# Scores written to the opposite partition half, and a strided unit's products alternated with newer scores

## The chip, the cores and the metric

The kernel runs on one core of a Trainium2 chip. The metric is device time in microseconds for one execution. Several executions are timed, and one more is recorded by the hardware profiler; line numbers such as L316 are lines of the kernel before, unless a text says that they are those of the changed kernel.

## The reference

The reference computes sparse attention for 8 batches of 8 heads (576 positions, head dimension 64), and feeds the result, as 4608 tokens of 512 values, to a two-layer network with g = h·cos(h) between the layers.

```python
def _attn_ref(q, k, v):
    stride = 32
    scores = scale * np.matmul(q, k.transpose(0, 1, 3, 2))
    mask_local = (rel >= 0) & (rel < stride)
    mask_strided = (rel >= 0) & (pos[None, :] % stride == pos[:, None] % stride)
    masks = np.stack([mask_local if h < H // 2 else mask_strided for h in range(H)], axis=0)
    ...
    return np.matmul(attn, v)

def _moe_ref(x, w_in, w_out):
    h = x @ w_in
    g = h * np.cos(h)
    return g @ w_out
```

Four heads of a batch are local: a query sees the 32 newest positions. Four are strided: a query sees the earlier positions of its own residue modulo 32.

## The kernel before

**The network** is most of the work. Tokens are taken in 12 blocks of 384 (j), the hidden width of 2048 in 16 chunks of 128 (f). A chunk's first layer is 12 matmuls into the tile h (L358), its second layer 9 matmuls into three accumulators acc (L382); the second layer of a chunk is issued three chunks after its first layer (LAG). Between them ACT, DVE and POOL make g_hi and g_lo from h (L364 to L375). All inputs of a block come from xT, a scratch in HBM that the attention writes.

**Attention** is cut into units, ten for each batch. For each pair of heads there are two strided units and three local ones. A unit has three steps on TensorE, separated by yield in the code:

- scores: q times k into the scores bank (L290 strided, L249 local), then the softmax on DVE, POOL and ACT, which ends with POOL's product into pn_s or e_sb (L225);
- transposes: three matmuls with an identity (L302 strided, L257 local), then ACT copies them to pt;
- products: v times pt into the products bank (L316 strided, L265 local), then ACT copies them to x_t (L322, L328) or x_l, from where a DMA takes them to xT.

All these matmuls have fp32 operands. A strided unit holds six groups of 54 positions (the second unit of a pair of heads holds five): 12 or 10 score matmuls and 12 or 10 product matmuls. A local unit has 6 and 6.

**Partition halves.** A score matmul contracts over the 64 values of a head, so it reads one half of the partitions: half 0 (0 to 63) or half 1 (64 to 127). A local unit has one head in each half (j); a strided unit has even groups in half 0 and odd groups in half 1 (i). Before, the scores are written to the same half as they are read from. The products of a strided unit read the 54 keys of head j from half j and write half j. The products of a local unit read 96 partitions, across both halves, and write half j. A matmul that reads from half a and writes half b is said below to be in quarter (a,b): before, all scores and all strided products are in (0,0) or (1,1).

**What sets the order.** Batches 0 and 1 come first, together with the loading of the weights (`plain` units). There a scheduler in the build decides the order on every engine. The other six batches, 60 units, are laid between the network's chunks from token block 2 on. There every matmul is chained to the one before it (in_turn, L147), so that TensorE's order is the order of the code. Before chunk n the units that fall due there (KNOTS, L58) form a burst: for unit k the transposes of unit k-2, then the products of unit k-3, then the scores of unit k (schedule, L416). In this part there is one bank of PSUM for scores, one for transposes and one for products. Of ten bursts for a batch, four have the products of a strided unit: their scores are those of the pair's last strided unit once (10 matmuls) and of local units three times (6 matmuls).

Of the kernel before, what the change touches and what calls it, by code (L numbers as in the profile page):

```python
# [3 lines left out]

# [17 lines left out]
STRIDE = 32  # L22
DM, DFF = H * D, 2048
NTOK = B * S
P = 128

QB = 64
# [41 lines left out]
def attention_cos_ffn(ctx, tc, qkl, vl, qkvs, w_in, w_out, eye, eye16, mask_l0, mask_l, mask_s, out):  # L69
# [26 lines left out]
        nc.gpsimd.memset(t, 0.0)  # L96
    exps, reduced = [], []

    def order(later, first, reason):
        tc.add_manual_dep(  # L100
            later.ins, first.ins.name,
            mybir.DependencyInfo(mybir.DependencyClass.NoSync, mybir.DependencyReason.DATA), reason=reason,
        )
# [49 lines left out]
        return mm  # L153

    class Attention:

# [77 lines left out]
        def local(self, b, p, u):  # L236
            qk = self.ld.tile([P, QS + KS], F32, name="qk")
            nc.sync.dma_start(out=qk[:, :QKL], in_=qkl[b, p, u])
            v = self.ld.tile([P, VS], F32, name="v", bufs=4)
            nc.sync.dma_start(out=v[:KW], in_=vl[b, p, u])  # L240
            q_t, k_t = qk[:, :LU * QB], qk[:, LU * QB:]
            v_t = v[:KW].rearrange("k (t j d) -> k t j d", j=2, d=D)
            mask = ml0.rearrange("p (t w) -> p t w", w=KW) if u == 0 else ml.unsqueeze(1).broadcast_to([P, LU, KW])
            s_ps = self.score_bank(mask)
            for t in range(LU):
                for j in range(2):
                    rows = slice(64 * j, 64 * j + 64)
                    lo = STRIDE if u + t == 0 else 0
                    self.scored = self.pe(nc.tensor.matmul(  # L249
                        s_ps[rows, t * KW + lo:(t + 1) * KW], q_t[rows, QB * t:QB * (t + 1)],  # L250
                        k_t[rows, QB * t + lo:QB * t + KW], start=not self.plain, stop=True, skip_group_check=True,
                    ))
            pn = self.softmax(s_ps[:, :LU * KW].rearrange("p (t w) -> p t w", w=KW), mask, LU, KW)
            yield
            t_ps = self.bank(self.transposed)
            for t in range(LU):
                self.pe(nc.tensor.transpose(t_ps[:KW, t * P:(t + 1) * P], pn[:, t], ident))  # L257
            pt = self.wk.tile([P, LU * P], F32, name="pt")
            nc.scalar.copy(out=pt[:KW], in_=t_ps[:KW, :LU * P])
            yield  # L260
            x_t = self.wk.tile([P, LU * QB], F32, name="x_l", bufs=4 if self.plain else 2)
            a_ps = self.bank(self.products)
            for t in range(LU):
                for j in range(2):
                    self.pe(nc.tensor.matmul(  # L265
                        a_ps[64 * j:64 * j + 64, t * QB:(t + 1) * QB], v_t[:, t, j],
                        pt[:KW, t * P + 64 * j:t * P + 64 * j + QB], start=True, stop=True, skip_group_check=True,
                    ))
            nc.scalar.copy(out=x_t, in_=a_ps[:, :LU * QB])
            at = b * S + u * LU * QB  # L270
            nc.scalar.dma_start(out=xT[:, 2 + p, at:at + LU * QB], in_=x_t)

        def strided(self, b, p, u):
            real = min(SU, NG - SU * u)
            qk = self.ld.tile([P, QS + KS], F32, name="qk")
            nc.sync.dma_start(out=qk, in_=qkvs[b, p, u, :, :QS + KS])
            v = self.ld.tile([P, VS], F32, name="v", bufs=4)
            nc.sync.dma_start(out=v[:, :real * D], in_=qkvs[b, p, u, :, QS + KS:QS + KS + real * D])
            q_t = qk[:, :QS].rearrange("p (t q) -> p t q", q=GB)
            k_t = qk[:, QS:].rearrange("p (t k) -> p t k", k=GB)  # L280
            v_t = v.rearrange("p (t d) -> p t d", d=D)

            mask = ms.unsqueeze(1).broadcast_to([P, SU, GB])
            s_ps = self.score_bank(mask)
            for t in range(SU):
                for i in range(2):
                    if SU * u + t // 2 * 2 + i >= NG:
                        continue
                    rows = slice(64 * i, 64 * i + 64)
                    self.scored = self.pe(nc.tensor.matmul(  # L290
                        s_ps[64 * i:64 * i + GB, t * GB:(t + 1) * GB], q_t[rows, t], k_t[rows, t],
                        start=not self.plain, stop=True, skip_group_check=True,
                    ))
            pn = next(self.pn_s)
            self.softmax(
                s_ps[:, :SU * GB].rearrange("p (t w) -> p t w", w=GB), mask,
                SU, GB, pn[:, :, :GB],
            )
            yield
            t_ps = self.bank(self.transposed)  # L300
            for t in range(0, SU, 2):
                self.pe(nc.tensor.transpose(  # L302
                    t_ps[:, t * GP:(t + 2) * GP], pn[:, t:t + 2].rearrange("p t k -> p (t k)"), ident
                ))
            pt = self.wk.tile([P, LU * P], F32, name="pt")
            nc.scalar.copy(
                out=pt[:, :SU * GB].rearrange("p (t q) -> p t q", q=GB),
                in_=t_ps[:, :SU * GP].rearrange("p (t q) -> p t q", q=GP)[:, :, :GB],
            )
            yield  # L310
            x_t = self.stage((b, p))
            a_ps = self.bank(self.products)
            for t in range(real):
                for j in range(2):
                    keys = slice(64 * j, 64 * j + GB)
                    self.pe(nc.tensor.matmul(  # L316
                        a_ps[64 * j:64 * j + 64, t * GB:(t + 1) * GB], v_t[keys, t],
                        pt[keys, t * GB:(t + 1) * GB], start=True, stop=True, skip_group_check=True,
                    ))
            x_v = x_t.rearrange("p (a r) -> p a r", r=STRIDE)  # L320
            full = min(real, STRIDE // GR - SU * u)
            nc.scalar.copy(  # L322
                out=x_v[:, :, GR * SU * u:GR * (SU * u + full)].rearrange("p a (t r) -> p t a r", r=GR),
                in_=a_ps[:, :full * GB].rearrange("p (t a r) -> p t a r", a=A, r=GR),
            )
            if full < real:
                left = STRIDE % GR
                nc.scalar.copy(  # L328
                    out=x_v[:, :, STRIDE - left:],
                    in_=a_ps[:, full * GB:real * GB].rearrange("p (a r) -> p a r", r=GR)[:, :, :left],  # L330
                )
            if u == NSU - 1:
                nc.scalar.dma_start(out=xT[:, p, b * S:(b + 1) * S], in_=x_t)
# [79 lines left out]
                steps.setdefault(stage, []).append(unit)  # L413
        return steps

    def schedule(units, begun, lag):  # L416


        steps = {}
        for k, at in enumerate(begun):  # L420
            steps.setdefault(at, []).extend(units[m] for m in (k - lag, k - lag - 1, k) if 0 <= m < len(units))
        return steps

    def step(steps, n):
        for unit in steps.get(n, ()):
            next(unit, None)

    with ExitStack() as loading:
        cv = loading.enter_context(tc.tile_pool(name="cv", bufs=2))
        with ExitStack() as stack:  # L430
# [17 lines left out]

            keep_busy(BUSY[0], None)
            for n in range(max(steps) + 1):  # L450
                step(steps, n)
                if n + 1 < len(BUSY):
                    keep_busy(BUSY[n + 1], att.scored)
                if n == LOADS[0]:
                    x0 = load_x(0)
                if n == LOADS[1]:
                    x1 = load_x(1)
# [21 lines left out]
    with ExitStack() as stack:  # L479
        op = stack.enter_context(tc.tile_pool(name="op", bufs=3, reuse_waits="tile"))  # L480
        ps = stack.enter_context(tc.tile_pool(name="ps", bufs=1, space=bass.MemoryType.PSUM, reuse_waits="tile"))
        att = Attention(stack, False, *(((ps, f"acc{i}"),) for i in range(3)), ld_bufs=2)
        units = [unit for b in range(2, B) for unit in att.units(b)]
        begun = np.interp(range(len(units) + UNIT_LAG + 1), [n for _, n in KNOTS], [at for at, _ in KNOTS])
        steps = schedule(units, begun.astype(int).tolist(), UNIT_LAG)
        for n in range(LAG, (NTB - 2) * NFC):
            j, f = 2 + n // NFC, n % NFC
            if f == 0:
                cur, acc = nxt, accumulators(ps_o)
            step(steps, n)  # L490
            if f == LOAD_AT and j + 1 < NTB:
                nxt = load_x(j + 1)
            chunk(j, f, cur, acc)
        while pend:
            outer(*pend.pop(0))
# [97 lines left out]
```

## Time and profile before

| | us |
|---|---|
| median of 3 runs | 1000.85 (1000.22 to 1001.1) |
| the profiled execution's own time | 999.46 |
| its span, first to last instruction | 997.7 |
| first layer's matmuls (L358), busy | 267.9 + 259.7 + 259.4 |
| second layer's matmuls (L382), busy | 227.4 + 224.2 + 224.6 |
| strided products (L316), busy, 704 records | 27.8 |
| local products (L265), busy, 576 records | 27.0 |
| local scores into acc banks (L249), 64 and 96 columns, busy | 4.2 + 25.8 |
| strided scores into acc banks (L290), busy, 572 records | 21.1 |

Busy times of a line are a union of its records, and matmuls overlap, so the rows of this table add up to more than the span. PE is TensorE's matmuls and PEld its weight loads; each matmul of fp32 operands appears as two records of each. The start of a record is measured; its end is modelled, so the text works with the distance from one start to the next. In a timeline, records of one line that follow one another are merged, with their count behind an x.

### The profile page before, as it was taken

The page shows a single profiled execution, that of the slowest core. Times are in us where ns is not written, and L with a number is a line of the kernel's source. Part 1 is how long each engine was busy: PE and PEld are TensorE (multiplying, and loading weights), DVE is VectorE, ACT ScalarE, POOL GpSimd, SP SyncE. Part 2 cuts the span into 40 slices and gives each one's busy share as a digit, 9 for nine tenths or more (in the row PEclk, how much of TensorE's full clock was granted, in tenths as well). Part 3 has the DMA queues.
Part 4 walks back from the last instruction along what each step waited for, and adds up shares of the span by engine and source line. Part 5 has one row for each costly group of instructions (what it writes and reads, how often), then busy time and mean ns, then how long its engine had stood idle before and what let it go on. Part 6 is the DMA issues. An engine that isn't in the chain of part 4 may idle for free.

```text
span 997.7 us, 17749 instructions
## 1 busy us (share of the span) xinstructions
PE 968.3 (97%) x6890; PEld 847.5 (85%) x6890; DVE 466.5 (47%) x1005; ACT 499.2 (50%) x1043; POOL 385.2 (39%) x418
## 2 busy tenths in 40 slices
PE   8988988998999999999999999999999999999998
PEld 5777877877888888888888888888888888889997
DVE  6866677655454444434344444444344444322222
ACT  3655555565555555455445545554454544433433
POOL 2555554544344344333333344434243333332221
PEclk9999999999899999999999999999999999999999
DMA  8963333232322222111211322211221310100000
GB/s 247 300 199 103 111 108 112 80 105 73 102 85 88 70 79 84 42 50 59 83 58 35 110 79 76 82 50 53 88 59 34 98 55 29 41 20 1 33 1 32
DMA packets 48228, 80.14 MB, mean 80 GB/s; under 512 B 5904, under 2 KB 33296, under 8 KB 48144
## 3 DMA queue, kind: packets, MB, share of 16 engines
q1 hardware_dynamic: 38208, 69.35, 23.1%
q10 hardware_dynamic: 9936, 9.65, 2.8%
q8 instruction: 54, 0.88, 0.4%
q14 instruction: 30, 0.25, 0.1%
HBM read 60.11 MB, written 18.87 MB: 79 GB/s over the span
## 4 chain that ended last, share of the span: by engine, by line
PE 78%; DMA 4%; DVE 2%; ACT 1%; issue 1%; POOL 0%; DVEq 0%; POOLq 0%; ACTq 0%; SPq 0%
PE h L358 35%; PE acc L382 34%; DMA raw<-in_w_out 2%; PE acc L249 2%; PE acc L265 2%; PE acc L316 2%; PE acc L290 2%; PE acc L257 1%; PE acc L302 1%; DVE raw L116 1%; DMA raw<-in_w_in 1%; DMA xT<-x_t 0%; ACT r L368 0%; DVE r L371 0%; DVE raw L119 0%
## 5 line engine op out<-in xcount | busy, mean ns | idle before, releaser
L375 POOL TENSOR_TENSOR g_lo<-r,g_hi 128x384 fp32r<-128x384 f32 x192 | 198.3, 1033 | 396.6 <-issue 249.2
L358 PE MATMUL h<-x_hi,wi_h 128*128 128x384 f32 x768 | 267.9, 349 | 13.7 <-DVE r L371 13.7
L358 PE MATMUL h<-x_hi,wi_l 128*128 128x384 f32 x768 | 259.7, 338 | 0.0
L358 PE MATMUL h<-x_lo,wi_h 128*128 128x384 f32 x768 | 259.4, 338 | 0.0
L365 DVE SCALAR_TENSOR_TENSOR r<-r,h 128x384 f32<-128x384 int32 x192 | 106.1, 552 | 270.8 <-ACT r L364 247.7
L382 PE MATMUL acc<-wo_l,g_hi 128*128 128x512 f32 x576 | 227.4, 395 | 0.0
L382 PE MATMUL acc<-wo_h,g_hi 128*128 128x512 f32 x576 | 224.2, 389 | 1.4 <-ACT g_hi L374 1.4
L382 PE MATMUL acc<-wo_h,g_lo 128*128 128x512 f32 x576 | 224.6, 396 | 0.0
L358 PEld LDWEIGHTS h<-x_hi,wi_h 128*128 128x128 f32 x768 | 145.2, 189 | 31.0 <-DVE r L371 19.8
L368 ACT ACTIVATE r<-r,quarter 128x384 f32<-128x384 f32 x192 | 118.5, 617 | 96.5 <-DVE r L365 96.2
L358 PEld LDWEIGHTS h<-x_lo,wi_h 128*128 128x128 f32 x768 | 145.3, 189 | 5.0
L371 DVE TENSOR_TENSOR r<-r,h 128x384 f32<-128x384 f32 x192 | 106.0, 552 | 84.0 <-ACT r L368 83.4
L358 PEld LDWEIGHTS h<-x_hi,wi_l 128*128 128x128 f32 x768 | 145.1, 189 | 0.1
L364 ACT ACTIVATE r<-h 128x384 int32<-128x384 f32 x192 | 93.4, 487 | 102.0 <-PE h L358 95.5
L374 ACT CAST g_hi<-r 128x384 fp32r<-128x384 f32 x192 | 98.3, 512 | 87.5 <-DVE r L371 87.2
L382 PEld LDWEIGHTS acc<-wo_h,g_lo 128*128 128x128 f32 x576 | 108.0, 188 | 22.8
L382 PEld LDWEIGHTS acc<-wo_h,g_hi 128*128 128x128 f32 x576 | 108.3, 188 | 19.0 <-ACT g_hi L374 1.7
L382 PEld LDWEIGHTS acc<-wo_l,g_hi 128*128 128x128 f32 x576 | 108.0, 187 | 18.2
L349 POOL TENSOR_TENSOR x_lo<-x_raw,x_hi 128x384 fp32r<-128x384 f32 x48 | 50.9, 1062 | 130.9 <-DVE x_hi L348 107.4
L214 ACT ACTIVATE e_sb<-t_sb,shift 128x288 f32<-128x288 f32 (+1 forms) x60 | 32.9, 548 | 95.6 <-POOL t_sb L206 95.6
L348 DVE CAST x_hi<-x_raw 128x384 fp32r<-128x384 f32 x48 | 21.6, 452 | 60.9 <-DMA x_raw<-xT 60.2
L206 POOL TENSOR_TENSOR t_sb<-t_sb,mx 128x288 f32<-128x288 f32 (+1 forms) x60 | 41.6, 693 | 16.9 <-DVE mx L205 11.5
(66 smaller groups left out, 855.8 us busy)
## 6 DMA issues: line engine op xcount, KB each, us to landing
qk<-in_qkvs SPq DMA_DIRECT2D x32, 324.0 KB, 3.7
qk<-in_qkl SPq DMA_DIRECT2D x48, 208.0 KB, 3.3
x_raw<-xT SPq DMA_DIRECT2D x48, 192.0 KB, 2.4
out<-o SPq DMA_DIRECT2D x36, 256.0 KB, 2.1
raw<-in_w_in SPq DMA_DIRECT2D x16, 512.0 KB, 3.7
raw<-in_w_out SPq DMA_DIRECT2D x16, 512.0 KB, 3.8
v<-in_vl SPq DMA_DIRECT2D x48, 144.0 KB, 2.2
xT<-x_t ACTq DMA_DIRECT2D x16, 288.0 KB, 3.5
```

Source lines behind the costliest of these rows:

```text
L206: nc.gpsimd.tensor_tensor(out=t, in0=t, in1=mx[:, :n].unsqueeze(2).broadcast_to([P, n, w]), op=ALU.subtract)
L214: nc.scalar.activation(out=e, in_=t, func=AF.Silu, bias=shift1, scale=0.0625)
L348: nc.vector.tensor_copy(out=hi, in_=raw)
L349: nc.gpsimd.tensor_tensor(out=lo, in0=raw, in1=hi.bitcast(F32), op=ALU.subtract)
L358: mm = nc.tensor.matmul(h, w[:, f, c], x[c], start=(i == 0), stop=(i == len(ops) - 1))
L364: nc.scalar.activation(out=k, in_=h, func=AF.Copy, scale=1.0 / (2.0 * math.pi), bias=0.25)
L365: red = nc.vector.scalar_tensor_tensor(out=r, in0=k, scalar=-2.0 * math.pi, in1=h, op0=ALU.mult, op1=ALU.add)
L368: sin = nc.scalar.activation(out=r, in_=r, func=AF.Sin, bias=quarter)
L371: nc.vector.tensor_tensor(out=r, in0=r, in1=h, op=ALU.mult)
L374: nc.scalar.copy(out=g_hi, in_=r)
L375: nc.gpsimd.tensor_tensor(out=g_lo, in0=r, in1=g_hi.bitcast(F32), op=ALU.subtract)
L382: mm = nc.tensor.matmul(acc[t], g[:, ts], w[:, f], start=(f == 0 and i == 0), stop=(f == NFC - 1 and i == 2))
```

## The change

Three edits, all to attention:

- A score matmul that reads half a writes half 1-a, for local and for strided units, in the first two batches too. So all scores are in quarters (0,1) and (1,0). The products then take their columns of pt from where the swapped scores end up after the transposes: the other half's columns for a local unit, those of the neighbouring group (t ^ 1) for a strided one. The products stay in the quarters that they had.
- A unit no longer issues its scores and products itself. It yields a list of them, with a mark that says whether the unit is strided.
- The new function burst takes the place of schedule and step for the last six batches. It issues the transposes as before. If the products are those of a strided unit, it alternates products and scores, matmul by matmul, until one list is used up, and then issues the rest. Otherwise it issues the products and then the scores, as before.

```diff
+    def half(n, rows=64):
+        return slice(64 * n, 64 * n + rows)
...
-            for t in range(LU):
-                for j in range(2):
-                    rows = slice(64 * j, 64 * j + 64)
-                    lo = STRIDE if u + t == 0 else 0
-                    self.scored = self.pe(nc.tensor.matmul(
-                        s_ps[rows, t * KW + lo:(t + 1) * KW], q_t[rows, QB * t:QB * (t + 1)],
...
+            def score(t, j):
+                lo = STRIDE if u + t == 0 else 0
+                self.scored = self.pe(nc.tensor.matmul(
+                    s_ps[half(1 - j), t * KW + lo:(t + 1) * KW], q_t[half(j), QB * t:QB * (t + 1)],
+                    k_t[half(j), QB * t + lo:QB * t + KW], start=not self.plain, stop=True, skip_group_check=True,
+                ))
+
+            yield [partial(score, t, j) for t in range(LU) for j in range(2)], False
...
-                        pt[:KW, t * P + 64 * j:t * P + 64 * j + QB], start=True, stop=True, skip_group_check=True,
...
+                at = t * P + 64 * (1 - j)
+                self.pe(nc.tensor.matmul(
+                    a_ps[half(j), t * QB:(t + 1) * QB], v_t[:, t, j], pt[:KW, at:at + QB], start=True, stop=True,
...
+                    s_ps[half(1 - i, GB), t * GB:(t + 1) * GB], q_t[half(i), t], k_t[half(i), t],
...
+            def product(t, j):
+                at = (t ^ 1) * GB
+                self.pe(nc.tensor.matmul(
+                    a_ps[half(j), t * GB:(t + 1) * GB], v_t[half(j, GB), t], pt[half(j, GB), at:at + GB], start=True,
+                    stop=True, skip_group_check=True,
+                ))
+
+            yield [partial(product, t, j) for t in range(real) for j in range(2)], True
...
+    def burst(transposed, multiplied, scored):
+
+        if transposed:
+            next(transposed)
+        products, small = next(multiplied) if multiplied else ((), False)
+        scores = next(scored)[0] if scored else ()
+        if small:
+            matmuls = [m for pair in itertools.zip_longest(products, scores) for m in pair if m]
+        else:
+            matmuls = [*products, *scores]
+        for matmul in matmuls:
+            matmul()
+        if multiplied:
+            next(multiplied, None)
+        if scored:
+            next(scored)
...
+            for units in bursts.get(n, ()):
+                burst(*units)
```

The first place is TensorE's order in the first burst of the last part that has the products of a strided unit. Here acc_2613, acc_2620 and acc_2456 are the banks of transposes, products and scores, and h and acc_2325 belong to the network. Before:

```order
L382 MATMUL acc_2325<-wo_h,g_lo 128x512
L302 MATMUL acc_2613<-ident,pn_s_97 128x128 x3
L316 MATMUL acc_2620<-pt,v 64x54 x12
L290 MATMUL acc_2456<-qk 54x54 x10
L358 MATMUL h<-x_hi,wi_h 128x384
```

And in the changed kernel, where L327 are the strided products, L297 the strided scores and L371 the first layer:

```order
L313 MATMUL acc_2613<-ident,pn_s_97 128x128 x3
L327 MATMUL acc_2620<-pt,v 64x54
L297 MATMUL acc_2456<-qk 54x54
L327 MATMUL acc_2620<-pt,v 64x54
L297 MATMUL acc_2456<-qk 54x54
...
L327 MATMUL acc_2620<-pt,v 64x54 x2
L371 MATMUL h<-x_hi,wi_h 128x384
```

The two blocks of 12 and 10 have become ten alternations with two products behind them; what stands ahead of and behind the burst is the same.

The second place is TensorE's order in the next burst, whose scores are those of a local unit (two matmuls of 64 columns and four of 96, L254 in the changed kernel):

```order
L313 MATMUL acc_2694<-ident,pn_s_96 128x128 x3
L327 MATMUL acc_2700<-pt,v 64x54
L254 MATMUL acc_2456<-qk 64x64
...
L327 MATMUL acc_2700<-pt,v 64x54
L254 MATMUL acc_2456<-qk 64x96
...
L327 MATMUL acc_2700<-pt,v 64x54 x4
```

Six scores alternate with the first six of ten products; the last four products come alone.

The third place is in the first two batches, where the scheduler decides. It is TensorE's order around the transposes of the first local units (acc_388, acc_428) and the scores into h and acc_604. Before:

```order
L257 MATMUL acc_388<-ident,e_sb 96x128
L316 MATMUL acc_374<-pt,v 64x54 x10
L257 MATMUL acc_388<-ident,e_sb 96x128 x2
L184 LDWEIGHTS ident_78
L184 MATMUL acc_604<-ms,ident_78 128x324
L257 MATMUL acc_428<-ident,e_sb 96x128 x3
L290 MATMUL h<-qk 54x54 x12
```

And in the changed kernel:

```order
L264 MATMUL acc_388<-ident,e_sb 96x128 x3
L327 MATMUL acc_374<-pt,v 64x54 x10
L190 LDWEIGHTS ident_78
L190 MATMUL acc_604<-ms,ident_78 128x324
L264 MATMUL acc_428<-ident,e_sb 96x128 x3
L297 MATMUL h<-qk 54x54 x10
L273 MATMUL acc_419<-pt,v 64x64 x6
```

Whole groups have moved by a few places against each other; none was added or left out. Similar small moves stand on DVE, ACT, POOL and SP in the first two blocks of the network, and single casts and loads of later blocks have moved past one or two neighbours.

More of the change, by code (lines that the diff above doesn't have):

```diff
@@ L3 @@
 from contextlib import ExitStack
+from functools import partial
 import ml_dtypes
@@ L244, in local @@
             s_ps = self.score_bank(mask)
-            for t in range(LU):
-                for j in range(2):
-                    rows = slice(64 * j, 64 * j + 64)
-                    lo = STRIDE if u + t == 0 else 0
-                    self.scored = self.pe(nc.tensor.matmul(
-                        s_ps[rows, t * KW + lo:(t + 1) * KW], q_t[rows, QB * t:QB * (t + 1)],
-                        k_t[rows, QB * t + lo:QB * t + KW], start=not self.plain, stop=True, skip_group_check=True,
-                    ))
+            def score(t, j):
[5 more added lines that the diff above has]
+            yield [partial(score, t, j) for t in range(LU) for j in range(2)], False
             pn = self.softmax(s_ps[:, :LU * KW].rearrange("p (t w) -> p t w", w=KW), mask, LU, KW)
@@ L262, in local @@
             a_ps = self.bank(self.products)
[L263 to L266, printed above, removed]
-                        pt[:KW, t * P + 64 * j:t * P + 64 * j + QB], start=True, stop=True, skip_group_check=True,
-                    ))
+            def product(t, j):
+                at = t * P + 64 * (1 - j)
+                self.pe(nc.tensor.matmul(
+                    a_ps[half(j), t * QB:(t + 1) * QB], v_t[:, t, j], pt[:KW, at:at + QB], start=True, stop=True,
+                    skip_group_check=True,
+                ))
+            yield [partial(product, t, j) for t in range(LU) for j in range(2)], False
             nc.scalar.copy(out=x_t, in_=a_ps[:, :LU * QB])
@@ L284, in strided, with score @@
             s_ps = self.score_bank(mask)
[L285 to L293, printed above, removed]
+            def score(t, i):
+                self.scored = self.pe(nc.tensor.matmul(
+                    s_ps[half(1 - i, GB), t * GB:(t + 1) * GB], q_t[half(i), t], k_t[half(i), t],
+                    start=not self.plain, stop=True, skip_group_check=True,
+                ))
+            yield [
+                partial(score, t, i) for t in range(SU) for i in range(2) if SU * u + t // 2 * 2 + i < NG
+            ], True
             pn = next(self.pn_s)
@@ L312, in strided, with product @@
             a_ps = self.bank(self.products)
[L313 to L319, printed above, removed]
+            def product(t, j):
+                at = (t ^ 1) * GB
+                self.pe(nc.tensor.matmul(
+                    a_ps[half(j), t * GB:(t + 1) * GB], v_t[half(j, GB), t], pt[half(j, GB), at:at + GB], start=True,
+                    stop=True, skip_group_check=True,
+                ))
+            yield [partial(product, t, j) for t in range(real) for j in range(2)], True
             x_v = x_t.rearrange("p (a r) -> p a r", r=STRIDE)
@@ L414, in in_stages, with stage @@
         return steps
[L416 to L425, printed above, removed]
-            next(unit, None)
+    def stage(unit):
+        matmuls = next(unit)
+        if matmuls:
+            for matmul in matmuls[0]:
+                matmul()
+            next(unit, None)
+    def burst(transposed, multiplied, scored):
[8 more added lines that the diff above has]
+        for matmul in matmuls:
+            matmul()
+        if multiplied:
+            next(multiplied, None)
+        if scored:
+            next(scored)
     with ExitStack() as loading:
@@ L450, in attention_cos_ffn @@
             for n in range(max(steps) + 1):
-                step(steps, n)
+                for unit in steps.get(n, ()):
+                    stage(unit)
                 if n + 1 < len(BUSY):
@@ L484, in attention_cos_ffn @@
         begun = np.interp(range(len(units) + UNIT_LAG + 1), [n for _, n in KNOTS], [at for at, _ in KNOTS])
-        steps = schedule(units, begun.astype(int).tolist(), UNIT_LAG)
+        bursts = {}
+        for k, at in enumerate(begun.astype(int).tolist()):
+            bursts.setdefault(at, []).append(
+                [units[m] if 0 <= m < len(units) else None for m in (k - UNIT_LAG, k - UNIT_LAG - 1, k)]
+            )
         for n in range(LAG, (NTB - 2) * NFC):
@@ L489, in attention_cos_ffn @@
                 cur, acc = nxt, accumulators(ps_o)
-            step(steps, n)
+            for units in bursts.get(n, ()):
+                burst(*units)
             if f == LOAD_AT and j + 1 < NTB:
```

## The prediction

> **What bounds the kernel now.** I read the page first, then the busy time by stretches, then TensorE's timeline in one batch of bursts.
>
> ```profile
> span 997.7 us, 17749 instructions
> PE 968.3 (97%) x6890; PEld 847.5 (85%) x6890; DVE 466.5 (47%) x1005; ACT 499.2 (50%) x1043; POOL 385.2 (39%) x418
> ```
> ```profile
> 50.00:205.00 155.00, 139.32 (x741) 120.93 (x737) 102.88 (x163) 85.09 (x161) 82.08 (x69) 0.99 0.37 117
> 205.00:262.00 57.00, 50.77 (x436) 44.59 (x435) 28.37 (x68) 32.60 (x69) 22.26 (x27) 0.94 0.31 95
> 262.00:900.00 638.00, 638.00 (x4582) 566.73 (x4582) 273.43 (x620) 319.36 (x685) 237.12 (x269) 1.00 0.22 65
> ```
>
> The second fence's columns are the stretch, its length, then busy time of PE, PEld, DVE, ACT and POOL, the granted clock, and DMA. From 262 to 900 us TensorE is busy for all of 638 us, so there a TensorE slot saved is time saved. From 205 to 262 it idles 6.2 us, and the clock is not full all the time; there a saving may end in a wait. Before 205 us nothing is interleaved.
>
> Busy says nothing of how well matmuls overlap. That shows in the distances between starts. These are the four bursts of one batch in which strided products stand ahead of scores, each up to the network's next matmul:
>
> ```profile
> 300.98 0.91 PE L316 MATMUL acc<-pt,v 54*64 54x54 f32 x24
> 301.72 0.76 PE L290 MATMUL acc<-qk 64*54 64x54 f32 x20
> 302.41 0.44 PE L358 MATMUL h<-x_hi,wi_h 128*128 128x384 f32 x1
> ...
> 311.29 0.79 PE L316 MATMUL acc<-pt,v 54*64 54x54 f32 x20
> 311.91 0.62 PE L249 MATMUL acc<-qk 64*64 64x64 f32 x12
> 312.47 0.44 PE L358 MATMUL h<-x_hi,wi_h 128*128 128x384 f32 x1
> ...
> 321.34 0.91 PE L316 MATMUL acc<-pt,v 54*64 54x54 f32 x24
> 322.08 0.62 PE L249 MATMUL acc<-qk 64*64 64x64 f32 x12
> 322.64 0.44 PE L358 MATMUL h<-x_hi,wi_h 128*128 128x384 f32 x1
> ...
> 331.53 0.79 PE L316 MATMUL acc<-pt,v 54*64 54x54 f32 x20
> 332.15 0.67 PE L249 MATMUL acc<-qk 64*64 64x96 f32 x12
> 332.75 0.44 PE L358 MATMUL h<-x_hi,wi_h 128*128 128x384 f32 x1
> ```
>
> Call them a to d. From the first product to the network they take 1.43, 1.18, 1.30 and 1.22 us, 5.13 us for a batch; the products' own parts are 0.74, 0.62, 0.74 and 0.62, the scores' 0.69, 0.56, 0.56 and 0.60. Twenty-four such bursts, six batches, are all that the alternation touches.
>
> **How two quarters share TensorE now.** Twelve product matmuls are 24 records, ten are 20: 0.12 us less for four records, so records leave two in about 0.06 us. I call that a slot. Which two? Two more places tell. First, strided scores behind the same kind of neighbour, with 24 and with 20 records:
>
> ```profile
> 281.26 0.80 PE L290 MATMUL acc<-qk 64*54 64x54 f32 x20
> 281.99 0.44 PE L358 MATMUL h<-x_hi,wi_h 128*128 128x384 f32 x1
> ...
> 291.37 0.81 PE L290 MATMUL acc<-qk 64*54 64x54 f32 x24
> 292.11 0.45 PE L358 MATMUL h<-x_hi,wi_h 128*128 128x384 f32 x1
> ```
>
> Twenty take 0.73 us, as long as 24 with 0.74. The 20 belong to units of five groups, whose last two matmuls read the same half: eight matmuls in two quarters need 8 slots, and the last four records, all in one quarter, 4 more, 12 as for the 24. So a slot passes one record of each of two quarters, and a quarter's second record doesn't hold up the other quarter, though it stands ahead of it in the program. Second, the local products, cut at three moments:
>
> ```profile
> 361.69 0.28 PE L265 MATMUL acc<-pt,v 96*64 96x64 f32 x2
> ...
> 361.69 0.34 PE L265 MATMUL acc<-pt,v 96*64 96x64 f32 x4
> ...
> 361.69 0.39 PE L265 MATMUL acc<-pt,v 96*64 96x64 f32 x6
> ...
> 362.19 0.71 PE L249 MATMUL acc<-qk 64*64 64x96 f32 x12
> ```
>
> Up to 361.79 us two records have started, up to 361.85 four, up to 361.91 six: two for each 0.06 us once the first slot, of 0.10, is over. Both read the same 96 partitions and write different halves. So sharing what they read doesn't keep two streams apart. Sharing the half that they write, as quarter (0,0) of a product and (1,0) of a score will, is shown nowhere before the change.
>
> **The change, part by part.**
>
> *Swapping the scores' halves* alone adds and removes no instruction; two quarters stay two quarters. I cost it at nothing, bounded by one slot (0.06 us) either way for each unit.
>
> *Alternating.* If four quarters run as two do, the scores pass beside the products. The burst is then the products plus the passage to the network. The local products show what a passage costs: 12 records, six slots of 0.06, are 0.36 us, but the next block starts 0.50 later, so 0.14, of which 0.04 is the longer first slot, already in the products' 0.74 and 0.62. I take 0.10. The bursts become 0.84, 0.72, 0.84 and 0.72, and save 0.59, 0.46, 0.46 and 0.50: **2.01 us for a batch**. That is the upper end. The lower comes from slots of unlike length. Six slots of 96-column scores take 0.60 less the passage, 0.083 each against 0.06. If a late score holds up the products that stand behind it, b and c lose four times 0.023, d six times, and a two slots of 0.05 for the two scores in one quarter: 0.43 together, which leaves **1.58**. The trace doesn't show how far a quarter may run ahead, so I take the middle, **1.8**.
>
> *What is hidden.* The rows of 262 to 900 us show no wait of TensorE that the saving could fall into, so five batches give 5 × 1.8 = 9.0. A score's wait for its q and k or for its bank would now hold the products too; there is none in this stretch. Work that waits for TensorE (DVE's mask add, ACT's copy of the products) starts up to 0.6 us sooner or at the same distance from the burst's start; those engines are half idle.
>
> The first batch is different:
>
> ```profile
> 238.49 0.27 ACT x_t L322
> ...
> 238.86 3.52 DMA xT<-x_t
> ...
> 242.44 2.35 DMA x_raw<-xT
> ...
> 247.20 0.63 POOL e_sb L225
> ...
> 247.87 0.88 PE acc L257 x3
> ```
> ```profile
> PE acc L257 <- POOL e_sb L225: 3.1, 1, 3.1
> ```
> ```profile
> 244.00:250.00 6.00, 2.90 (x51) 2.34 (x49) 2.40 (x6) 2.01 (x5) 3.19 (x4) 0.82 0.28 77
> 250.00:256.00 6.00, 6.00 (x30) 5.56 (x29) 2.48 (x8) 2.10 (x6) 1.36 (x3) 0.61 0.45 142
> ```
> ```profile
> 248.68 1.32 PE L316 MATMUL acc<-pt,v 54*64 54x54 f32 x20
> ...
> 250.90 0.69 PE L358 MATMUL h<-x_hi,wi_h 128*128 128x384 f32 x1
> ```
>
> The chain of waits runs from ACT's copy after burst b through a store, a load and POOL, which works in order, to the transposes at 247.87, for which TensorE waits 3.1 us. Only what burst a saves (0.5) moves this chain; b and c are swallowed, the wait grows by their 0.8. Burst d then runs at a granted clock of about half and takes 2.22 us; twice the new 0.72 to 0.86 saves 0.6. So the first batch gives about 1.1, not 1.8. A longer idle time may also move the slow stretch: the clock's shortfall in the two rows is 6 × 0.18 + 6 × 0.39 = 3.4 us of work, and I allow half of it, 1.7, either way.
>
> *The first 205 us* are reordered by the scheduler. They have 13.7 us of waits of the first layer in 12 pieces:
>
> ```profile
> PE h L358 <- DVE r L371: 13.7, 12, 3.0
> ```
>
> Weights arrive there late whatever the units do, so I take nothing, and one average piece, 1.1 us, either way.
>
> **Sum.** 9.0 + 1.1 = 10.1 us off the profiled execution's 999.46, of which the span is 997.7. The median of the runs is 1.4 above it, so 1000.85 − 10.1 = **990.8**. With 1.58 to 2.01 for a batch, and the two allowances, the forecast's own range is 987 to 994.5.
>
> **Rivals.**
>
> *Two at a time.* No row of before shows more than two records in a slot. If that is a limit, or if streams that write one half shut each other out, the 44 records of burst a still need 22 slots, as 12 + 12 less two now, and nothing or 0.1 us is gained in a burst: 998.5 to 1001. For it: nothing shows a third stream. Against it: neither reading halves nor order in the program kept the two streams apart, and products and scores write different banks.
>
> *The loads collide: slower.* If a weight load can't pass beneath a running matmul of another quarter that reads the same half, each record costs the unhidden first slot, 0.10 us, in its half. Bursts a to d have 24, 16, 18 and 16 records in the fuller half: 7.4 us against 5.13 now, 2.3 more for a batch, 13.6 in all: about 1014. It decides from 5.13/74 = 0.069 us for a record on. For it: first slots do take 0.10. Against it: the local products read the same partitions and pass two in 0.06.
>
> The Trainium skill, page "TensorE: Matmul & The Clock Gate", section "The mechanism", states this rule: weight loads overlap running matmuls only where the row group differs. By that rule this rival's 1014 would come out. The trace disagrees, by those local products. The same page's section "Measured speedup vs the span model" gives a speedup of 10.6 for 16 packed tiles, which would mean that streams with a common output half do overlap, and the upper end of the forecast; no run here shows it.
>
> *The clock or the early wait costs more than it does now.* Two slow stretches like the one above in place of one would take back 3.4 us: 994 to 996, still faster. That the alternation isn't there can be left out: TensorE's order is chained in this part.
>
> **How the numbers follow.** Forecast 75%, the forecast with a worse early stretch 4%, two at a time 13%, loads collide 6%, another loss 2%. A measurement of this kernel tells about 0.2%, 2 us, from no change. Faster by more than that: the first two, and a small part of the third, 0.80; within: 0.12; slower: 0.08. The range takes the forecast's lower end and reaches up past the early loss to the edge of the second rival: 986.5 to 998.
>
> **What would show it.** The alternated records of L327 with L297 or L254 in a to d should last about 0.72 to 0.95 us to the network's next matmul, in place of 1.2 to 1.4. The wait for e_sb near 247 us should grow to about 4 us. If the bursts last as long as now, two at a time is right; if over 1.5, the loads collide. If the bursts shrink and the time doesn't, I was wrong about what hides behind them; a change ahead of 205 us would be the scheduler's.

## The result and the profile after

| | before | changed kernel |
|---|---|---|
| median, us | 1000.54 (4 runs, 996.7 to 1001.1) | 986.46 (4 runs, 985.43 to 988.69) |
| the profiled execution's own time | 999.46 | 985.93 |
| its span | 997.7 | 984.1 |
| first score of the last six batches, us from the span's start | 216.39 | 215.05 |
| from there to the end | 781.3 | 769.1 |

The ratio is 0.9886, with a 95% interval of 0.9865 to 0.9908. The forecast was 990.8 with a range of 986.5 to 998: its mechanism holds, and the gain is larger than forecast: the median lies at the lower edge of the range.

The page of the changed kernel has nearly the instructions of before, and TensorE is as busy as ever:

```profile
span 984.1 us, 17763 instructions
PE 954.8 (97%) x6890; PEld 833.9 (85%) x6890; DVE 467.9 (48%) x1005; ACT 499.6 (51%) x1043; POOL 384.4 (39%) x418
```

The same three stretches as before (length, then busy time of PE, PEld, DVE, ACT and POOL, granted clock, DMA share and rate):

```profile
50.00:205.00 155.00, 140.42 (x752) 120.79 (x746) 107.62 (x167) 87.83 (x168) 83.34 (x72) 1.00 0.36 117
205.00:262.00 57.00, 50.34 (x466) 43.98 (x466) 29.60 (x74) 33.32 (x72) 22.16 (x28) 0.94 0.31 98
262.00:900.00 638.00, 638.00 (x4614) 567.02 (x4613) 273.44 (x618) 322.94 (x688) 238.69 (x272) 1.00 0.21 65
```

From 262 to 900 us TensorE still has no idle time at full clock, but 4614 matmul records fit where 4582 did. A share of busy time says nothing of this gain; distances between starts do. This is TensorE's timeline over burst a of a late batch. Lines have moved by the edit: L327 are the strided products, L297 the strided scores, L254 the local scores, L371 the first layer.

```profile
297.41 0.26 PE L327 MATMUL acc<-pt,v 54*64 54x54 f32 x1
297.42 0.25 PE L297 MATMUL acc<-qk 64*54 64x54 f32 x1
297.43 0.26 PE L327 MATMUL acc<-pt,v 54*64 54x54 f32 x1
297.43 0.29 PE L297 MATMUL acc<-qk 64*54 64x54 f32 x2
297.51 0.22 PE L327 MATMUL acc<-pt,v 54*64 54x54 f32 x1
...
298.04 0.29 PE L327 MATMUL acc<-pt,v 54*64 54x54 f32 x4
298.26 0.44 PE L371 MATMUL h<-x_hi,wi_h 128*128 128x384 f32 x1
```

Each matmul is two records, so program order is product, product, score, score. The starts are not in that order: product, score, product, score within 0.02 us, one record for each of the four quarters, and the next round 0.1 us after the first. Bursts b, c and d, each from its first product to the network:

```profile
307.13 0.26 PE L327 MATMUL acc<-pt,v 54*64 54x54 f32 x1
...
307.86 0.44 PE L371 MATMUL h<-x_hi,wi_h 128*128 128x384 f32 x1
```
```profile
316.73 0.26 PE L327 MATMUL acc<-pt,v 54*64 54x54 f32 x1
...
317.58 0.44 PE L371 MATMUL h<-x_hi,wi_h 128*128 128x384 f32 x1
```
```profile
326.45 0.26 PE L327 MATMUL acc<-pt,v 54*64 54x54 f32 x1
...
327.18 0.45 PE L371 MATMUL h<-x_hi,wi_h 128*128 128x384 f32 x1
```

With burst a's 0.85 these are 0.73, 0.85 and 0.73 us, where before had 1.43, 1.18, 1.30 and 1.22. The table gives the means over the last five batches, for this kernel and for those of the experiments that change the bursts; the others have the changed kernel's lengths within 2 ns.

| from first product to network, ns | a | b | c | d | sum |
|---|---|---|---|---|---|
| before | 1430 | 1178 | 1294 | 1226 | 5128 |
| changed kernel | 843 | 726 | 844 | 727 | 3140 |
| halves swapped, in blocks | 1250 | 997 | 1113 | 1046 | 4406 |
| alternated, halves as before | 1430 | 1219 | 1335 | 1270 | 5254 |
| by twos | 837 | 720 | 837 | 721 | 3115 |
| by fours | 849 | 720 | 836 | 720 | 3125 |
| by eights | 1016 | 880 | 881 | 929 | 3706 |
| scores left out | 837 | 720 | 837 | 720 | 3114 |

A batch saves 1.99 us. The span's 13.5 us (from 997.68 to 984.14) are then: 9.9 in the five batches, 2.3 in the first batch, and 1.3 ahead of it (the table at the top). The first batch's chain of waits, to set against the one shown before:

```profile
236.98 0.28 ACT x_t L335
...
237.35 2.71 DMA xT<-x_t
...
240.12 2.33 DMA x_raw<-xT
...
244.87 0.63 POOL e_sb L231
...
245.54 0.88 PE acc L264 x3
```
```profile
PE acc L264 <- POOL e_sb L231: 3.6, 1, 3.6
```

The wait for e_sb grew from 3.1 to 3.6 us. Counted from the first score of this part, the transposes behind it come at 30.49 us in place of 31.48.

### The profile page after: what moved, and what is told of

Read it like the earlier page. It is cut to its first block, busy times and chain, and to the rows that moved or that the text cites. A ratio compares the mean times of both kernels' runs of the same rounds, so it can differ in the third digit from the quotient of the medians.

```text
span 984.1 us, 17763 instructions
## 1 busy us (share of the span) xinstructions
PE 954.8 (97%) x6890; PEld 833.9 (85%) x6890; DVE 467.9 (48%) x1005; ACT 499.6 (51%) x1043; POOL 384.4 (39%) x418
## 4 chain that ended last, share of the span: by engine, by line
PE 77%; DMA 2%; DVE 2%; ACT 2%; issue 1%; POOL 1%; POOLq 0%; DVEq 0%; ACTq 0%; SPq 0%
PE h L371 35%; PE acc L395 34%; PE acc L273 2%; PE acc L254 2%; DMA raw<-in_w_out 1%; PE acc L297 1%; PE acc L264 1%; PE acc L327 1%; PE acc L313 1%; DVE raw L120 1%; DVE raw L129 0%; ACT raw L128 0%; DVE r L378 0%; POOL g_lo L388 0%; DMA xT<-x_t 0%
## 5 line engine op out<-in xcount | busy, mean ns | idle before, releaser
L371 PE MATMUL h<-x_hi,wi_h 128*128 128x384 f32 x768 | 267.1, 348 | 14.6 <-DVE r L384 14.6
L371 PE MATMUL h<-x_hi,wi_l 128*128 128x384 f32 x768 | 259.3, 338 | 0.0
L371 PE MATMUL h<-x_lo,wi_h 128*128 128x384 f32 x768 | 258.8, 337 | 0.0
L371 PEld LDWEIGHTS h<-x_hi,wi_h 128*128 128x128 f32 x768 | 144.7, 188 | 31.5 <-DVE r L384 21.6
L371 PEld LDWEIGHTS h<-x_lo,wi_h 128*128 128x128 f32 x768 | 144.7, 188 | 5.0
L371 PEld LDWEIGHTS h<-x_hi,wi_l 128*128 128x128 f32 x768 | 144.5, 188 | 0.3 <-POOL wi_l L134 0.3
L212 POOL TENSOR_TENSOR t_sb<-t_sb,mx 128x288 f32<-128x288 f32 (+1 forms) x60 | 41.8, 696 | 10.1 <-DVE mx L211 8.5
```

The source lines that it names most:

```text
L212: nc.gpsimd.tensor_tensor(out=t, in0=t, in1=mx[:, :n].unsqueeze(2).broadcast_to([P, n, w]), op=ALU.subtract)
L371: mm = nc.tensor.matmul(h, w[:, f, c], x[c], start=(i == 0), stop=(i == len(ops) - 1))
```

## The experiments

Ten kernels ran, each beside the kernel before on the same chip; short diffs are against the changed kernel. The first four take the change apart and vary its grain.

**Halves swapped, in blocks.**

```diff
-        if small:
+        if False:
```

> The scores' halves swapped, the bursts in blocks as before (products, then scores). Theory Q (four quarters run at once, but only if their matmuls stand close together in the program): bursts a to d last 1.43, 1.18, 1.30 and 1.22 us less at most one or two slots of 0.06, so the time falls by 0 to 3 us, of which up to 1.3 may come from the new order of the first 205 us, which this kernel has too. Rival O (the alternating order alone makes the gain): no more than that 1.3. Rival R (TensorE looks far ahead in its queue): the swap alone lets the scores run beside the products, a to d under 1.0 us, time near 988.

Measured: 995.12 us, ratio 0.995 (0.9932 to 0.9968). TensorE's timeline in burst a:

```profile
300.23 0.73 PE L327 MATMUL acc<-pt,v 54*64 54x54 f32 x18
300.75 0.26 PE L297 MATMUL acc<-qk 64*54 64x54 f32 x2
300.80 0.23 PE L327 MATMUL acc<-pt,v 54*64 54x54 f32 x2
...
300.94 0.61 PE L297 MATMUL acc<-qk 64*54 64x54 f32 x14
301.48 0.44 PE L371 MATMUL h<-x_hi,wi_h 128*128 128x384 f32 x1
```

The swap alone was costed at nothing; it saves 0.18 us in every burst, three slots, where the expectation allowed two. The first scores start when 18 of the 24 product records have started, so six, three for each quarter, are still to come. TensorE's weight loads (PEld) show where these three are: the load for the first of them begins together with that for the first score.

```profile
300.75 0.12 PEld L297 LDWEIGHTS acc<-qk 64*54 64x54 f32 x1
300.75 0.14 PEld L327 LDWEIGHTS acc<-pt,v 54*64 54x64 f32 x1
```

So in each quarter one record runs, one loads its weights, and two wait. What has been issued waits for its quarter, and the records of other quarters pass it.

**Alternated, with the halves as before.**

```diff
-                    s_ps[half(1 - i, GB), t * GB:(t + 1) * GB], q_t[half(i), t], k_t[half(i), t],
+                    s_ps[half(i, GB), t * GB:(t + 1) * GB], q_t[half(i), t], k_t[half(i), t],
...
-                at = (t ^ 1) * GB
+                at = t * GB
```

The local units are changed back in the same way.

> The alternation without the swap: scores and products in the same two quarters, first two batches in the order of before. Theory Q: 44 and 32 records still need 22 to 24 and 16 slots, bursts a to d last 1.2 to 1.5 us as before, the time is that of before within 2 us. Rival O (the order alone makes the gain): a to d fall to 0.7 to 0.9 us, the time to 987 or 988.

Measured: 999.76 us, ratio 0.9998 (0.9972 to 1.0024). The same place:

```profile
300.66 0.33 PE L327 MATMUL acc<-pt,v 54*64 54x54 f32 x4
300.82 0.27 PE L297 MATMUL acc<-qk 64*54 64x54 f32 x4
300.92 0.32 PE L327 MATMUL acc<-pt,v 54*64 54x54 f32 x4
301.03 0.30 PE L297 MATMUL acc<-qk 64*54 64x54 f32 x4
```

Products and scores follow one another, four records in two slots, as in the blocks of before. Bursts b to d are even 0.04 us longer. So the order alone gains nothing, the halves alone gain 0.72 us for a batch, and both together 1.99: the gain is not a sum of two parts. Four quarters can run side by side, but a quarter's record must be near enough to the front of the program.

**By twos and by fours.** With N = 2 and N = 4:

```diff
-            matmuls = [m for pair in itertools.zip_longest(products, scores) for m in pair if m]
+            matmuls = []
+            for at in range(0, max(len(products), len(scores)), N):
+                matmuls += [*products[at:at + N], *scores[at:at + N]]
```

> As the changed kernel, but two products, then two scores. Four matmuls in a row still use all four quarters. Theory Q with a queue that passes over several waiting records: a to d as in the changed kernel (0.85, 0.73, 0.85, 0.73), time the same within 1 us. If a waiting record stops the stream almost at once: bursts 0.1 to 0.3 us longer each, time 2 to 6 us above the changed kernel.

> Four products, then four scores. Two products of one quarter (four records) now stand ahead of the first score. With a reach of a few records in each quarter: bursts between those of the changed kernel and of before, about 1.0 us for a and c and 0.85 to 1.0 for b and d, time 3 to 8 us above the changed kernel. With a far reach: as the changed kernel, within 1 us.

Measured: by twos 989.09 us, ratio 0.9882 (0.9836 to 0.9928), and by fours 987.36, ratio 0.9869 (0.9816 to 0.9921); both ratios are that of the whole change within their intervals. The bursts are those of matmul by matmul within 8 ns; the grain does not matter up to fours. From these four came a theory of how far a quarter runs ahead: TensorE issues in order, each quarter holds two records that wait, and issue stops when the next record's quarter is full. It gives the three slots of the swap alone if the two are counted behind the record whose weights load, as the rows above show (the expectation below says: behind the one that runs). By eights should stop the issue again.

**By eights**, the same edit with N = 8:

> Eight products, then eight scores, then the rest. Theory W (TensorE passes records on in program order, and each quarter holds two that wait behind the one that runs; only a third stops the stream): from slots of 0.058, 0.050 and 0.083 us and the passage, a to d come to 1.03, 0.90, 0.90 and 0.94 us. With three that wait: 0.98, 0.84, 0.84, 0.88. If there is no such limit: 0.84, 0.72, 0.84, 0.72. If the stream stops at the first that waits: 1.15, 0.95, 1.04, 1.00.

Measured: 991.95 us, ratio 0.9937 (0.9913 to 0.9961), with bursts of 1.02, 0.88, 0.88 and 0.93 us. The start of burst a:

```profile
300.65 0.50 PE L327 MATMUL acc<-pt,v 54*64 54x54 f32 x10
300.93 0.26 PE L297 MATMUL acc<-qk 64*54 64x54 f32 x2
```

Ten of the first 16 product records have started when the first score does: again three of each quarter are left, one that loads and two that wait. All four bursts lie within 0.02 us of what the expectation gives for two waiting records; its times for three waiting, for none and for no limit are off by up to 0.05, 0.16 and 0.21.

**The first two batches as before**, where the swap alone applies:

```diff
-                    s_ps[half(1 - i, GB), t * GB:(t + 1) * GB], q_t[half(i), t], k_t[half(i), t],
+                    s_ps[half(i if self.plain else 1 - i, GB), t * GB:(t + 1) * GB], q_t[half(i), t], k_t[half(i), t],
```

The other three places are changed likewise.

> The last six batches as in the changed kernel, the first two batches with the scores in the old halves, so that TensorE's order there is that of before. Theory Q (all of the gain is in the bursts): first 205 us as spread as in the other runs, bursts as in the changed kernel, ratio 0.987 to 0.990. Rival R (1.3 us of the gain come from the scheduler's new order ahead of 205 us): ratio 0.990 or more, and the last part begins near 216.4 us, as before, not near 215.

Measured: 987.13 us, ratio 0.988 (0.986 to 0.99); the last six batches start at 217.76 us and take 768.9. The time is that of the whole change; the swap in the first two batches is worth nothing that can be measured. Nor is the 1.3 us ahead of the last part the scheduler's: over all profiled executions that part starts at 213.8 to 217.9 us, and the changed kernel, run again (below), at 215.39.

**Local products alternated too.** Their list is marked like that of a strided unit:

```diff
-            yield [partial(product, t, j) for t in range(LU) for j in range(2)], False
+            yield [partial(product, t, j) for t in range(LU) for j in range(2)], True
```

> The products of local units, which read 96 partitions across both halves, alternate with the scores too (36 more bursts). If a change between these and 64-row scores must wait until TensorE has run empty, as the 0.10 to 0.14 us between the two blocks of before suggest, some ten changes more for a burst add about 1 us to each: time 1020 to 1040. If they overlap as quarters do, these bursts fall from 1.14 and 1.24 to 0.7 to 0.9 us and the time by up to 10 us more.

Measured: 1091.08 us, ratio 1.0922 (1.0886 to 1.0958). Bursts a to d keep their length. Of the 36 others, the 33 that have scores behind the products take 3.1 to 3.6 us where they took 1.14 to 1.24; the last three have products alone, and stay at 0.50. One of them (L273 are the local products):

```profile
293.60 0.33 PE L273 MATMUL acc<-pt,v 96*64 96x64 f32 x2
293.86 0.30 PE L297 MATMUL acc<-qk 64*54 64x54 f32 x2
294.09 0.33 PE L273 MATMUL acc<-pt,v 96*64 96x64 f32 x2
```

Here nothing passes anything: a product takes 0.26 us to the next start, a score 0.23, where two records of one matmul in its own quarter take two slots, 0.12. At full clock these bursts lose 1.9 to 2.2 us, twice the 1 us expected, with 11 changes of kind in place of one: 0.2 us for each of the ten more. The 33 bursts have grown by 72 of the 102 us that the last part grew; with the rest goes a mean granted clock of 0.957 in place of 0.997. So matmuls that lie within one quarter each run beside one another; one over 96 partitions shuts scores out, and they it. That the array drains between the two shapes is argued, not shown; its price is shown.

**Scores left out.** The scores of the 24 bursts are not computed; the softmax works on what the bank holds.

```diff
-            matmuls = [m for pair in itertools.zip_longest(products, scores) for m in pair if m]
+            matmuls = products
```

> The scores of the 24 bursts with strided products are left out: the softmax works on what an earlier unit left in the bank. Theory Q (the scores run wholly beside the products): a to d still last 0.84, 0.72, 0.84, 0.72, within 0.03, and the time is that of the changed kernel within 1 us. If the scores still cost part of a slot each, the bursts fall below 0.80 and 0.68 and the time by 1 to 3 us.

Measured: 982.36 us, ratio 0.9834 (0.9807 to 0.9861). Products alone, burst a:

```profile
292.26 0.91 PE L327 MATMUL acc<-pt,v 54*64 54x54 f32 x24
293.10 0.44 PE L371 MATMUL h<-x_hi,wi_h 128*128 128x384 f32 x1
```

They take 0.84 us, so in the changed kernel ten scores beside them cost 0.006 us: there is nothing left to gain here. The Trainium skill, page "TensorE: Matmul & The Clock Gate", section "The mechanism", says that weight loads overlap running matmuls only where the row group differs, and that matmuls start and end in program order. Neither is so here: scores and products that read the same half run in 0.84 us together, and their starts are out of order (ends are modelled, and can't tell). The gain of packing that the section "Measured speedup vs the span model" gives, 10.6 for 16 packed tiles, agrees with this in kind: four quarters at work take 0.84 us for what took two quarters 1.43.

The time is 4.1 us under the changed kernel's, where it was to be within 1. That is not the scores' own work, which 24 bursts at 0.006 us put at 0.1. The first batch shows no wait for e_sb: that softmax waits for no score of the bursts, and is done when TensorE comes. The transposes stand at 28.62 us from the first score, in place of 30.49, and burst d behind them runs at full clock, 0.72 us in place of 1.26. From the first score to the end this kernel takes 764.9 us, 4.2 less than the changed one.

**The load behind the softmax, and the changed kernel again.** Is that wait the load's, which stands ahead of e_sb on DVE and POOL? (att.inverse and att.normal keep each unit's reciprocal on DVE and last product on POOL; the lines that fill them are left out here.)

```diff
-            nc.vector.tensor_copy(out=hi, in_=raw)
-            nc.gpsimd.tensor_tensor(out=lo, in0=raw, in1=hi.bitcast(F32), op=ALU.subtract)
+            high = nc.vector.tensor_copy(out=hi, in_=raw)
+            low = nc.gpsimd.tensor_tensor(out=lo, in0=raw, in1=hi.bitcast(F32), op=ALU.subtract)
+            if unit is not None and c == 0:
+                order(high, att.inverse[unit], "behind the unit's softmax")
+                order(low, att.normal[unit], "behind the unit's softmax")
...
-                nxt = load_x(j + 1)
+                nxt = load_x(j + 1, 4 if j == 2 else None)
```

> The changed kernel with one thing moved: in the first batch, the cast x_hi on DVE and the difference x_lo on POOL of the first tile loaded for the next token block (which wait for the load from xT) stand behind the fifth unit's softmax (z and e_sb) instead of ahead of it. TensorE's order and SP's are the same. If the 3.6 us wait of TensorE for e_sb comes from DVE and POOL standing behind that load, e_sb no longer waits for the load: it was ready to run from about 242.3 us (ACT's square ends at 241.5, then 0.48 + 0.17 + 0.18 us on DVE), not 244.87, so the wait falls to about 1 us, 2.5 us of it go, and the last part takes about 766 us instead of 769.1; a ratio to the kernel before of about 0.984 to 0.985. If the wait belongs to the softmax's own chain from the scores (which leaving the scores out cut too), it stays at 3 us or more and the time is that of the changed kernel.

> The changed kernel itself, as a control beside the run before it on the same chip: 986.5 us within 2, a wait for e_sb of 3 to 4 us, and 769 us for the last part.

Measured: 986.33 us, ratio 0.9875 (0.9848 to 0.9902), against 986.47 for the changed kernel, ratio 0.987 (0.9847 to 0.9893): no difference. With the load behind the softmax, TensorE's wait, two rows of the chain of waits, and two of TensorE's timeline 20 us ahead of them (lines have moved by one to four again):

```profile
PE acc L265 <- POOL e_sb L232: 2.1, 1, 2.1
```
```profile
237.25 0.28 ACT x_t L336
...
243.53 0.79 POOL e_sb L232
```
```profile
224.93 0.52 PE L375 MATMUL h<-x_hi,wi_l 128*128 128x384 f32 x1
225.25 0.52 PE L375 MATMUL h<-x_hi,wi_h 128*128 128x384 f32 x1
```

From ACT's copy to e_sb it is 6.28 us, in place of 7.89 in both executions of the changed kernel. So the load is worth 1.6 us of the wait, not 2.5; the other 2.1 stay, with POOL's g_lo now ahead of e_sb. But in this execution TensorE lost 1.5 us ahead of the place that was moved, in a stretch with matmuls 0.32 us apart (0.17 at full clock), so the transposes stand at 30.54 us from the first score, where the changed kernel has 30.49 and, run again, 30.48. Whether the 1.6 us are a gain beneath the clock's scatter stays open; the times show none.

## Why the prediction was right, and where its terms were off

**Four quarters overlap** was the likeliest case, and holds: bursts a to d at 0.84, 0.73, 0.84 and 0.73 us against 0.84, 0.72, 0.84 and 0.72. The passage of 0.10 us to the network was right too: products alone take 0.837 and 0.720, of which 0.74 and 0.62 were their own part.

**1.8 us for a batch was too small; it is 1.99**, the upper end. The lower end came from late scores that hold up the products behind them. They don't: the products of b, c and d with late scores beside them take 0.006 to 0.007 us more than alone, since two records may wait in each quarter before TensorE's issue stops. The middle was taken because the trace of before did not show how far a quarter runs ahead. It makes 5 × 0.188 = 0.9 us.

**The swap at nothing, bounded by one slot,** was wrong in its reason as well as its size. It stood on two quarters staying two quarters, but at the seam between the blocks four quarters are open, and three slots of 0.06 us overlap. In the changed kernel this is no extra gain, since alternating takes the same overlap and more.

**The first batch gave 2.3 us, not 1.1.** The step that failed is that the chain of waits moves by burst a's 0.5 alone. The transposes at its end came 0.99 us sooner, and by another way. ACT's copy of the products moved by only 0.17, though burst b begins 0.56 sooner: ACT's copy to pt, two steps ahead of it, waited before for TensorE's transposes, and now waits for ACT's own square. The chain before, then in the changed kernel:

```profile
237.28 0.34 PE acc L302 x3
...
237.65 0.43 ACT pt L306
```
```profile
235.84 0.36 ACT e_sb L225
236.21 0.31 ACT pt L317
```

The rest came from the store behind the copy, which took 2.71 us in place of 3.52. The traces show what goes with that. SP issues the next loads of v, and of q and k, when burst b's products and scores are done, and the load of q and k stood right ahead of the store before (238.86), and 0.98 us ahead of it (237.35) in the changed kernel:

```profile
238.83 0.34 SPq L238 DMA_DIRECT2D qk<-in_qkl  x1
```
```profile
236.37 0.33 SPq L244 DMA_DIRECT2D qk<-in_qkl  x1
```

In the seven profiled executions whose bursts a to d have the changed kernel's length (within 8 ns), and which run this chain, that load stands 0.98 to 1.02 us ahead of the store, and the store takes 2.63 to 2.80. In the four with longer bursts the load stands 0.71, 0.57, 0.06 and 0.03 us ahead, and the store takes 3.00, 3.32, 3.59 and 3.52. So burst b's saving was not swallowed: it seems to have reached the chain through these loads. No run moved the loads alone, so that they hold up the store is argued, not shown.

Burst d was mis-sized too. At half clock it fell from 2.23 to 1.26 us: 0.97 against 0.6, because the forecast doubled a length of 0.72 to 0.86, and at half clock the burst took 1.7 times its 0.73. But the slow stretch is equally long in both executions (below), so what burst d no longer takes of it, other matmuls take; burst d's gain of its own is the 0.50 of full clock. That burst c is swallowed, and that the wait grows, was right (3.6 us; about 4 was forecast).

**The first 205 us at nothing** was right as to the scheduler: with the first two batches as before the time is the same. The 1.3 us there lie in the scatter of 213.8 to 217.9 us, which is wider than the 1.1 allowed.

**The clock** cost less than before, where 1.7 us were allowed either way. The windows around the slow stretch of the changed kernel:

```profile
240.00:245.00 5.00, 1.99 (x43) 1.53 (x41) 3.29 (x8) 2.59 (x6) 2.08 (x3) 0.89 0.38 111
245.00:250.00 5.00, 4.46 (x42) 3.99 (x43) 2.01 (x6) 2.59 (x7) 1.78 (x3) 0.50 0.25 79
250.00:255.00 5.00, 5.00 (x43) 4.18 (x43) 2.46 (x8) 2.71 (x7) 1.43 (x2) 0.92 0.29 95
```

5 × (0.11 + 0.50 + 0.08) are 3.4 us of clock lost, the 3.4 of before. But before, the slow stretch began with the transposes, and in the changed kernel its first 1.64 us fell into TensorE's wait (before, then changed):

```profile
247.87:254.70 6.83, 6.83 (x47) 6.24 (x48) 1.97 (x6) 3.29 (x8) 1.86 (x3) 0.50 0.38 117
```
```profile
243.90:245.54 1.64, 0.00 (x0) 0.00 (x0) 0.88 (x4) 0.00 (x0) 1.64 (x4) 0.51 0.10 37
```

Half of 1.64, 0.8 us, is therefore work not lost, an estimate from these two rows. With the chain's 0.99 and burst d's 0.50 it makes up the 2.3 of the first batch; that this stretch fell so is luck, and the second profiled execution of the changed kernel lost only 1.7 us to its own.

**The rivals.** Two at a time fell by the records above (four starts in 0.02 us, a burst of 0.84 where it asked for 1.4). The colliding loads, at over 1.5 us for a burst, fell by the same burst, and by the scores left out. Together, the sum of 10.1 us should have been 12.2 for the last part, 2.1 more: 0.9 in the five batches and 1.2 in the first. The 1.3 ahead of it is chance, and it helped to bring the time to the edge of the range.

## What to carry to other kernels

In these runs, streams of small matmuls (fp32, up to 96 columns, each within one half for reading and one for writing) take almost nothing from one another if no two of them both read and write the same halves of the partitions: give all four quarters work, and interleave finely enough that the two records which wait in a quarter last until its next one is issued. Interleaving within the same quarters gained nothing, and interleaving matmuls over 64 and over 96 partitions cost 0.2 us for each change. Count a saving on TensorE from the distances between starts, and look for the place where it falls into a wait.

## What the runs showed of the hardware that was not expected

- Each quarter of the array holds two records behind the one whose weights load, and later records of other quarters pass them. The swap alone overlaps three slots (0.18 us) at each seam; by eights all four bursts come out within 0.02 us of this count.
- Two streams of scores beside two of products, with every half read by two streams and written by two, cost 0.006 us in a burst of 0.84.
- A change between matmuls over 64 and over 96 partitions costs 0.2 us, 1.9 to 2.2 us for a burst with ten changes more; with the lower granted clock that came with it, 0.957, that kernel took 9.2% longer.
- A store took 2.63 to 2.80 us with a load issued 1.0 us ahead of it, and 3.52 and 3.59 with the load 0.03 and 0.06 ahead.
- In the first 262 us, stretches of TensorE at half clock, of 3.4 to 10.2 us, come and go: the two profiled executions of the changed kernel lost 3.4 and 1.7 us to them. A gain of such a size in that part can't be told from one execution.
